# Sends of routed rows in the experts' first blocks: two behind step seven, none at step six and behind step two

## The chip, the cores and the metric

The kernel runs on one core of a Trainium2 chip. The metric is the time of one launch on the device in microseconds (us), lower is better. A core has five engines that run side by side, each through its own instructions in order: TensorE (PE, with its weight loads shown apart as PEld), VectorE (DVE), ScalarE (ACT), GpSimd (POOL) and SyncE (SP). They wait for each other by semaphores. DMA transfers are issued here by SP, POOL and ACT.

## The reference

```python
def reference(**kwargs):
    # x: (8, 5056, 128), h: (5056, 128)
    Yf = rfft(x, n=2 * S, axis=1) * rfft(h, n=2 * S, axis=0)   # a long causal convolution
    x = irfft(Yf, n=2 * S, axis=1)[:, :S].reshape(40448, 128)
    g = argmax(x @ w_group)             # one of 4 groups, softmax weight g_w
    e = argmax(x @ w_expert[g])         # one of 4 experts in it, softmax weight e_w
    out[token] = g_w * e_w * (relu(x[token] @ w1[g, e]) @ w2[g, e])
```

Each of the 40448 rows of the convolution's result thus goes through one of 16 experts (128 to 1024 to 128), all in float32.

## The kernel before

**Two halves that overlap.** The convolution is done in three rounds of three sequences (`ROUNDS`; one of the nine is `h`). The end of a round, its last transform and the routing of its rows, is `side(r)`: eight parts, of which each has two *lumps* on PE, further pieces of PE work (logits, transposes: `lm`, `lt`, `rows`), some 40 small DVE steps (`gate_math`) and at its end 15 *sends* (10 in the first round). A lump (`lump`, L721 and L735) is 48 and 24 matmuls of small size into the banks `py0` and `py1`, which ACT then copies to `yT` (L742). The experts are worked off in blocks of 512 rows, gathered by expert in the DRAM tensor `srt`.

**A send.** `scatter` (from L849 on) makes a function for each column of 128 rows; `send` (L869) takes the oldest from the list `self.sends` and calls it, or does nothing if the list is empty. It casts one column of positions to integers (L853: on DVE, or on ACT if asked by `send("s")`) and then has POOL issue an indirect DMA that writes these rows to `srt` (L854). `drain` sends all that is left, with casts on DVE. `rows(0)` of a part first sends what is left of the parts before the last one.

**The order is written by hand.** `run` fills the list `main` with functions; their order is the order of emission, and so the order on each engine. The blocks of the experts come in eight steps each: `step(i)` of `ffn_steps` does three matmuls of the first layer for each 128 of the inner 1024 (L1350 to L1352), three of the second for an earlier step (L1368 to L1370), ACT and DVE take the result out of PSUM as `h` (L1355, L1356), and what `PLAN` lists for the place (`act`): splits of weights and rows, and under the letter "o" the store of results: at steps 4 and 6 of the first blocks a `put` and a `send("s")`, at 3 and 5 a `scatter_out` (POOL again, L1421).

**The weave.** `weave` walks through `main`. Only steps 2 and 6 of a block have a weight (`FW`), and the large pieces of `side(2)` are emitted by weight: right behind step 2 or step 6, ahead of the next entry of `main`. So a send that is an entry of its own behind step 2 (`k % 8 == 2`) is emitted behind the large piece that follows that step, while a send within step 6 is emitted ahead of the piece that follows it. In blocks 0 to 23 sixteen lumps are emitted in this way, the first behind step 6 of block 1, the other fifteen behind steps 2; behind the steps 6 of later blocks come the other large pieces. In numbers of steps, counted from step 0 of block 0, the lumps stand behind 14, 18, 34, 42, 58, 66, 82, 90 and so on by turns of 8 and 16 to 186.

**When the list fills.** At step 0 of block 0 the list holds 14 sends of the second round. The eight parts of the third round add 15 each behind steps 42, 66, 90, 111, 135, 158, 182 and 206. `drain` stands behind steps 15 and 255; the loads of rows behind it (`ffn_x`, L1253, by SP) wait for the scatters to have landed.

Of the kernel before, what the change touches and what calls it, by code (L numbers as in the profile page):

```python
# [81 lines left out]
NA = (NTOK_A - NE * (BLK - 1) + BLK - 1) // BLK  # L82
# [139 lines left out]
def width(j):  # L222

    return BLK if j < T0 else TB if j < H0 else HB


def steps_of(n):
    return 8 // (512 // n)


class Kernel:
# [1245 lines left out]
    def ffn_steps(self, j, prev, end):  # L1477

        n = width(j)
        ns = steps_of(n)  # L1480
        plan = PLAN[n]

        def bank(j):
            return (NW_MIN - 1 - j) % 2 if j < NW_MIN else 0

        def behind(i):

            if j < NW_MIN:
                return [i - 2]
            return [] if i < 3 else [ns - 4, ns - 3] if i == ns - 1 else [i - 3]  # L1490

        def loads_a():
            if j + 2 < end:
                self.ffn_x(j + 2)

        def loads_w():
            if j + 2 < end:
                self.ffn_w(j + 2)

        def act(at):  # L1500
            for w, k, q in plan:
                if w != at:
                    continue
                if q == "w":
                    loads_w()
                elif q == "s":
                    if prev:
                        self.out_store(
                            prev[0], self.blk[j - 1]["ids"] if prev[1] is None else prev[1], j - 1 if j < NW_MIN else None
                        )  # L1510
                elif q == "o":
                    if prev and j < NA - 2 and at in (4, 6):
                        self.put()
                        self.send("s")
                    elif prev:
                        self.scatter_out(1 if ns == 8 else 4, j < NW_MIN)
                elif j + k < end and (j + k, q) not in self.kept:
                    if q == "x":
                        self.ffn_prep_x(j + k)
                    else:  # L1520
                        self.ffn_prep_w(j + k, q)

        def step(i):
            def f():
                if i == 0:
                    loads_a()
                act(i - 0.5)
                if i >= 2 or j not in (T0, H0):
                    self.mm1(j, i)
                if i >= 2:  # L1530
                    for q in behind(i):
                        self.mm2(n, q, bank(j), j)
                elif prev:
                    self.mm2(prev[0], steps_of(prev[0]) - 2 + i, bank(j - 1))
                    if i == 1:
                        self.out_evac(prev[0], bank(j - 1))
                act(i)

            return f

        return [step(i) for i in range(ns)]
# [81 lines left out]
    def run(self):  # L1623
        tc = self.tc
        with ExitStack() as ctx:
            self.pools(ctx)
            with ExitStack() as c2:
# [10 lines left out]
                def add(f, w=0.0):  # L1638
                    main.append((w, f))
# [4 lines left out]
                def advance(g):  # L1644
                    return lambda: next(g, None)
# [50 lines left out]
                for k, f in enumerate(steps):  # L1696
                    for g in rest[LATE * k:LATE * k + LATE]:
                        add(g)
                    if k == 8 * (N0 - 2) - SIDE1:
                        mark["end", 1] = len(main)  # L1700
                    if k == START2 - 7:
                        add(side[2][0])
                    if k == START2:
                        mark["start", 2] = len(main)
                    if 8 * (N0 - 2) - SIDE1 < k:
                        for _ in range(NTA):
                            add(advance(ta))
                    if k == 8 * (NA - 2) - SIDE2:
                        mark["end", 2] = len(main)
                    if 8 * (NA - 2) - SIDE2 < k < 8 * NA:  # L1710
                        for _ in range(NTA):
                            add(advance(tq))
                    if 8 * NA <= k:
                        add(advance(tb))
                    if 8 * NA + FILL <= k:
                        add(advance(fill))
                    if 8 * NW_MIN - AHEAD <= k:
                        add(advance(ahead))
                    if k < 4:
                        add(lambda q=(0, 2, 1, 3)[k]: self.ffn_w(1, (q,)))  # L1720
                    add(f, FW[k % 8])
                    if k in (8 * (N0 - 2) - 1, 8 * (NA - 2) - 1):
                        add(self.drain)
                    elif k < 8 * (NA - 2) and k % 8 not in (3, 4, 5, 6):
                        add(lambda: self.send("s"))
                    elif k >= 8 * (NA - 2) and k % 8 in (7, 0, 1, 2):
                        add(lambda: self.scatter_out(1, True))
                    if k % 8 == 6:
                        add(lambda: (self.due.extend(self.taken), self.taken.clear()))
                    m, n = k // 8 - NA, (PUT1 - PUT0) // 2  # L1730
                    if k % 8 == 0 and 0 <= m < TAKE and (m + 1) * n // TAKE > m * n // TAKE:
                        add(lambda i=m * n // TAKE: self.take(i))
# [31 lines left out]
```

## Time and profile before

| | us |
|---|---|
| median of 3 runs | 1758.63 |
| shortest and longest of them | 1750.66, 1761.71 |
| the profiled execution | 1759.51 |
| its span, first to last instruction | 1757.7 |

The span is what the trace covers; the profiled execution's own time is 1.8 us more. Busy times are those of instructions on an engine. Matmuls overlap, and their ends are modelled, so a short wait between two of them can hide under the shown length of the first; where that matters, the length of a whole stretch is taken. "issue" as the cause of idle time means that the engine waited for nothing that the profile shows.

### The profile page before, as it was taken

To read this page: it belongs to the slowest core of one execution; us is meant where nothing else is said; L and a number is where in the kernel's file an instruction comes from. 1 tells how busy PE (TensorE), PEld (TensorE's weight loads), DVE (VectorE), ACT (ScalarE), POOL (GpSimd) and SP (SyncE) were. 2 spreads that over 40 slices of the span, in tenths; PEclk is the share of its full clock that TensorE was granted. 3 is DMA by queue.
4 is the path that set the end of the run, shared out by engine and by line. 5 is a ranking of instruction groups with operands and counts; after the bars stand their busy time and mean duration, and the time that the engine had idled before them with its cause. 6 is when DMAs were issued, how large, how long until landed. Compare 5 with 4: busy or idle time off the path is not lost. (4 is left out here: it accounts for less than half of the span.)

```text
span 1757.7 us, 48202 instructions
## 1 busy us (share of the span) xinstructions
PE 1661.5 (95%) x16765; PEld 1299.0 (74%) x16765; DVE 1297.0 (74%) x3080; ACT 1043.0 (59%) x2461; POOL 769.0 (44%) x742
## 2 busy tenths in 40 slices
PE   8998899988898998999999999999999999999997
PEld 8677756567655556777777778787788877888987
DVE  6554598864586787777777778887787778877876
ACT  5564444443343445666666666676666666666765
POOL 1451243442454454144455545254565554334444
PEclk9999999999998999999999999999999999999999
DMA  7796677876487777555665654447545584444554
GB/s 219 229 299 204 179 249 237 275 230 182 145 247 232 244 226 212 168 165 163 171 175 167 171 152 147 133 144 227 186 148 156 166 254 136 130 129 146 156 164 152
DMA packets 281640, 330.26 MB, mean 188 GB/s; under 512 B 33335, under 2 KB 216000, under 8 KB 281368
## 3 DMA queue, kind: packets, MB, share of 16 engines
q1 hardware_dynamic: 252504, 271.00, 52.2%
q0 software_dynamic: 20608, 41.79, 6.9%
q10 hardware_dynamic: 8256, 14.10, 2.8%
q8 instruction: 140, 2.29, 0.6%
q14 instruction: 132, 1.08, 0.2%
HBM read 230.41 MB, written 96.86 MB: 186 GB/s over the span
## 5 line engine op out<-in xcount | busy, mean ns | idle before, releaser
L854 POOL DMA_INDIRECT srt<-rw,pos x320 | 344.9, 1078 | 450.0 <-DVE pos L853 173.4
L1421 POOL DMA_INDIRECT out<-orow,at x176 | 182.2, 1035 | 254.4 <-ACT at L1419 200.8
L539 DVE TENSOR_TENSOR y<-pp,hg 128x768 f32<-128x768 f32 (+1 forms) x120 | 103.8, 865 | 79.1 <-ACT hg L529 31.1
L1421 POOL DMA_INDIRECT out<-orow,sids x92 | 94.0, 1022 | 116.8 <-DVE orow L1388 83.7
L589 PE MATMUL pp<-y,cg 64*64 64x384 f32 (+1 forms) x1472 | 118.7, 444 | 14.4 <-DVE m L539 10.6
L599 ACT COPY zs<-pp 128x768 f32<-128x768 f32 (+1 forms) x118 | 85.2, 722 | 79.2 <-PE pp L589 40.2
L439 DVE TENSOR_TENSOR st<-pp,odd 128x320 f32<-128x320 f32 x90 | 44.2, 491 | 104.3 <-ACT odd L438 102.4
L521 PE MATMUL pp<-st,cg 64*64 64x192 f32 (+1 forms) x1556 | 117.8, 407 | 0.8 <-issue 0.4
L721 PE MATMUL py<-ig,zm 126*64 126x79 f32 x2048 | 95.5, 243 | 18.7 <-issue 15.1
L721 PEld LDWEIGHTS py<-ig,zm 126*64 126x64 f32 x2048 | 82.1, 142 | 39.2 <-issue 28.0
L1356 DVE SCALAR_TENSOR_TENSOR h0l<-px,h0h 128x512 fp32r<-128x512 f32 (+1 forms) x109 | 73.5, 675 | 50.1 <-ACT h0h L1355 34.9
L742 ACT COPY yT<-py 128x474 f32<-128x474 f32 (+1 forms) x96 | 44.6, 513 | 106.2 <-PE py L735 86.6
L1355 ACT ACTIVATE h0h<-px 128x512 fp32r<-128x512 f32 (+1 forms) x109 | 63.9, 586 | 73.6 <-PE px L1352 47.3
L539 DVE TENSOR_TENSOR m<-pp,hg 128x768 f32<-128x768 f32 (+1 forms) x120 | 102.9, 858 | 1.2 <-ACT hg L531 1.2
L1356 DVE SCALAR_TENSOR_TENSOR h2l<-px,h2h 128x512 fp32r<-128x512 f32 (+1 forms) x112 | 75.5, 674 | 37.8 <-ACT h2h L1355 28.9
L589 PEld LDWEIGHTS pp<-y,cg 64*64 64x64 f32 x1472 | 59.2, 133 | 53.4 <-issue 26.7
L1356 DVE SCALAR_TENSOR_TENSOR h3l<-px,h3h 128x512 fp32r<-128x512 f32 (+1 forms) x111 | 74.6, 672 | 30.2 <-ACT h3h L1355 26.8
L521 PEld LDWEIGHTS pp<-st,cg 64*64 64x64 f32 x1556 | 62.9, 134 | 40.3 <-issue 33.6
L1355 ACT ACTIVATE h3h<-px 128x512 fp32r<-128x512 f32 (+1 forms) x111 | 65.2, 587 | 37.3 <-PE px L1352 27.1
L573 POOL TENSOR_TENSOR y<-y,m 128x512 f32<-128x512 f32 x40 | 51.0, 1276 | 74.5 <-DVE m L561 42.0
L1356 DVE SCALAR_TENSOR_TENSOR h1l<-px,h1h 128x512 fp32r<-128x512 f32 (+1 forms) x111 | 74.7, 673 | 8.3 <-issue 2.9
L1355 ACT ACTIVATE h1h<-px 128x512 fp32r<-128x512 f32 (+1 forms) x111 | 65.1, 587 | 22.1 <-PE px L1352 10.0
(476 smaller groups left out, 5187.4 us busy)
## 6 DMA issues: line engine op xcount, KB each, us to landing
wr<-in_moe_w SPq DMA_DIRECT2D x373, 256.0 KB
zd<-zs SPq DMA_DIRECT2D x78, 384.0 KB
zm<-zd SPq DMA_DIRECT2D x64, 378.0 KB
cg<-in_c_g SPq DMA_DIRECT2D x102, 224.0 KB
xr<-srt SPq DMA_DIRECT2D x71, 260.0 KB
hg<-hd SPq DMA_DIRECT2D x80, 128.0 KB
zd<-zs SPq DMA_DIRECT2D x39, 256.0 KB
xt<-in_x ACTq DMA_DIRECT2D x54, 160.0 KB
```

The lines of the kernel that those rows point to most:

```text
L439: nc.vector.tensor_tensor(out=all_st[:, 0:2 * HALF, d], in0=even, in1=odd, op=ALU.add)
L521: nc.tensor.matmul(px[c * 64:c * 64 + 64, b, to], lhsT=k, rhs=data[:, of], start=begin, stop=i == len(steps) - 1 or p == 0 and i == 1, til ...
L539: nc.vector.tensor_tensor(out=t[:, :, 0:w].rearrange("p t (r u d) -> p t r u d", r=2, u=nu), in0=taken(px, part).unsqueeze(1).broadcast_to ...
L573: (nc.gpsimd if r == 0 else nc.vector).tensor_tensor(out=y[:, :, 0:w], in0=y[:, :, 0:w], in1=m[:, :, 0:w], op=ALU.add)
L589: nc.tensor.matmul(pz[c][h:h + 64, 0:w], lhsT=wt[c * 64:c * 64 + 64, k + h:k + h + 64], rhs=y[c * 64:c * 64 + 64, part, 0:w], start=part = ...
L599: nc.scalar.copy(out=z[:, 0:n, 0:w], in_=pp[:, 0:n, 0:w])
L721: nc.tensor.matmul(pys[q][c:c + 64, col(n, u)], lhsT=zms[q][:, n % QB, k:k + 64], rhs=self.ig[:, 0:NH], start=n % QB == 0 and u == 0, stop ...
L742: nc.scalar.copy(out=self.yT[:, k:k + QB * c1], in_=pys.pop(q)[:, 0:QB * c1])
L854: ins = self.nc.gpsimd.indirect_dma_start(out=self.srt, out_offset=bass.IndirectOffsetOnAxis(ap=k["pos"][0:p, j:j + 1], axis=0), in_=k["rw ...
L1355: nc.scalar.activation(out=hh, in_=p, func=AF.Relu)
L1356: nc.vector.scalar_tensor_tensor(out=hl, in0=p, scalar=0.0, in1=hh.bitcast(F32), op0=ALU.max, op1=ALU.subtract)
L1421: ins = self.nc.gpsimd.indirect_dma_start(out=self.a["out"], out_offset=bass.IndirectOffsetOnAxis(ap=ids, axis=0), in_=o, in_offset=None, ...
```

## The change

One entry of `PLAN` keeps its `put` at step 6 and loses its send; behind step 2 there is no send any more; behind step 7 there are two. Where a list of sends is empty, a call does nothing, as before. So a block that follows another has five places for a send (7, 7, 0, 1 and within 4) where it had six (7, 0, 1, 2 and within 4 and 6).

```diff
                     if prev and j < NA - 2 and at in (4, 6):
                         self.put()
-                        self.send("s")
+                        if at == 4:
+                            self.send("s")
                     elif prev:
                         self.scatter_out(1 if ns == 8 else 4, j < NW_MIN)
...
                     add(f, FW[k % 8])
                     if k in (8 * (N0 - 2) - 1, 8 * (NA - 2) - 1):
                         add(self.drain)
-                    elif k < 8 * (NA - 2) and k % 8 not in (3, 4, 5, 6):
+                    elif k < 8 * (NA - 2) and k % 8 in (7, 0, 1):
                         add(lambda: self.send("s"))
+                        if k % 8 == 7:
+                            add(lambda: self.send("s"))
```

`N0` is 4 and `NA` is 34 here.

## Rows read from the trace of the kernel before

**Rows 1.** The page's first part: the span, and of each engine the busy time in us, its share of the span and the number of its instructions.

```profile
span 1757.7 us, 48202 instructions
...
PE 1661.5 (95%) x16765; PEld 1299.0 (74%) x16765; DVE 1297.0 (74%) x3080; ACT 1043.0 (59%) x2461; POOL 769.0 (44%) x742
```

**Rows 2.** Busy time of each engine by stretch (the windows view; us from the span's start; length of the stretch, then busy us and instruction count of PE, PEld, DVE, ACT, POOL, then granted clock, DMA share, GB/s): all before the turn to the experts, the stretch in which the last 120 sends run, and the stretch behind it.

```profile
0.00:652.00 652.00, 587.20 (x10344) 417.62 (x10348) 440.34 (x1152) 298.97 (x773) 253.01 (x254) 0.97 0.74 226
...
754.00:1092.00 338.00, 335.87 (x2372) 269.18 (x2371) 259.93 (x600) 230.85 (x575) 175.98 (x166) 1.00 0.58 164
1092.00:1500.00 408.00, 400.49 (x1872) 323.99 (x1871) 323.28 (x684) 281.66 (x652) 200.93 (x192) 1.00 0.56 170
```

**Rows 3.** Who PE waited for between 720 and 1095 us (the waits view: what waited, for whom, us in total, times, the longest in us); these four lines are the whole answer.

```profile
PE py L721 <- issue: 1.1, 3, 0.4
PE py L735 <- issue: 0.4, 1, 0.4
PE ptr L1370 <- DMA wr<-in_moe_w: 0.3, 1, 0.3
PE pz L1370 <- issue: 0.3, 1, 0.3
```

**Rows 4.** The windows view again, one stretch for each of the twelve lumps that had a scatter on POOL beside them: it begins with the lump's first L721 matmul and ends where PE takes up the next step (columns as in rows 2, so the fifth pair is the busy time of POOL in the lump and the count of its instructions that fall in it). The last line sums the columns.

```profile
694.04:697.95 3.91, 3.33 (x74) 2.69 (x73) 1.31 (x3) 0.71 (x4) 1.95 (x2) 1.00 0.79 255
703.63:707.42 3.79, 3.48 (x74) 2.64 (x73) 1.29 (x2) 0.64 (x3) 1.93 (x2) 1.00 0.18 54
779.35:782.77 3.42, 3.07 (x74) 2.56 (x73) 3.35 (x11) 0.86 (x2) 1.66 (x2) 1.00 0.29 72
825.34:828.79 3.45, 3.12 (x73) 2.63 (x72) 3.23 (x12) 0.65 (x2) 1.00 (x2) 1.00 0.33 75
871.64:874.40 2.76, 2.76 (x74) 2.45 (x73) 2.64 (x11) 0.07 (x1) 0.97 (x1) 1.00 0.28 64
886.60:889.46 2.86, 2.86 (x73) 2.55 (x72) 1.74 (x3) 1.53 (x4) 0.98 (x1) 1.00 0.51 117
917.10:920.04 2.94, 2.94 (x73) 2.56 (x72) 2.58 (x10) 0.09 (x1) 0.96 (x1) 1.00 0.29 68
932.43:935.84 3.41, 3.02 (x73) 2.64 (x73) 1.47 (x3) 0.93 (x2) 1.41 (x2) 1.00 0.17 51
962.96:966.04 3.08, 3.08 (x73) 2.63 (x72) 2.52 (x9) 0.54 (x2) 1.00 (x1) 1.00 0.34 68
978.30:981.81 3.51, 3.13 (x73) 2.62 (x72) 1.37 (x3) 0.82 (x2) 1.30 (x2) 1.00 0.32 72
1008.90:1011.80 2.90, 2.90 (x73) 2.55 (x72) 1.81 (x7) 0.82 (x3) 1.46 (x2) 1.00 0.31 93
1023.98:1027.11 3.13, 3.05 (x74) 2.59 (x73) 1.29 (x2) 0.59 (x2) 0.98 (x1) 1.00 0.22 72
sum 39.16, PE 36.73 PEld 31.11 DVE 24.61 ACT 8.26 POOL 15.62; mean PE 3.06 PEld 2.59 DVE 2.05 ACT 0.69 POOL 1.30
```

**Rows 5.** The same for the four lumps without one.

```profile
734.57:737.32 2.75, 2.75 (x73) 2.44 (x72) 2.63 (x7) 1.28 (x3) 0.00 (x0) 1.00 0.22 38
749.51:752.26 2.75, 2.75 (x73) 2.44 (x72) 1.29 (x2) 0.53 (x2) 0.00 (x0) 1.00 0.24 39
794.95:797.71 2.76, 2.76 (x73) 2.45 (x73) 1.29 (x2) 0.54 (x2) 0.00 (x0) 1.00 0.41 80
841.09:843.84 2.75, 2.75 (x73) 2.44 (x72) 1.29 (x2) 0.53 (x2) 0.00 (x0) 1.00 0.50 113
```

**Rows 6.** The timeline of POOL around the lump at 825.34 us (start, us, engine, line, operation, out<-in, count, and in brackets the idle time before it and what ended that), and under it PE's rows of the lump in the same view.

```profile
823.10 0.98 POOL L854 DMA_INDIRECT srt<-rw,pos  x1 [2.32 <-ACT pos L853]
...
825.67 0.98 POOL L854 DMA_INDIRECT srt<-rw,pos  x1 [0.31 <-issue]
...
825.35 1.72 PE L721 MATMUL py<-ig,zm 126*64 126x79 f32 x42
827.39 0.44 PE L721 MATMUL py<-ig,zm 126*64 126x79 f32 x6 [0.33 <-issue]
```

**Rows 7.** ACT and POOL between 754 and 1092 us: the groups of the casts and of the scatters (the lines view: count | busy us, mean ns of one | idle us before them and what ended it), and one line of the waits of ACT.

```profile
L853 ACT CAST pos<-posf 128x1 int32<-128x1 f32 x120 | 23.3, 194 | 5.2 <-DVE posf L985 5.2
...
L854 POOL DMA_INDIRECT srt<-rw,pos x120 | 131.4, 1095 | 108.8 <-ACT pos L853 59.2 <-issue 19.3 <-DVE kept_ids L1398 9.7
...
ACT h0h L1355 <- PE px L1352: 10.8, 15, 2.2
```

**Rows 8.** The drain behind step 15: the timeline of POOL (first and last of its four scatters), of SP (the load of block 4's rows and the first load of its weights) and of ACT (the first use of those weights).

```profile
700.61 0.98 POOL L854 DMA_INDIRECT srt<-rw,pos  x1 [4.17 <-DVE pos L853]
...
704.69 1.17 POOL L854 DMA_INDIRECT srt<-rw,pos  x1 [0.31 <-issue]
...
707.39 0.37 SPq L1253 DMA_DIRECT2D xr<-srt  x1
708.60 0.37 SPq L1286 DMA_DIRECT2D wr<-in_moe_w  x1
...
725.01 0.61 ACT L1297 CAST w0h<-wr 128x512 fp32r<-128x512 f32 x1
```

**Rows 9.** DMA queues in the lump that begins at 825.34 us up to the end of its gap (its first line: the scatters' queue), then in the one that begins at 794.95 us (the instructions' queue): packets, MB, share of 16 engines.

```profile
q0 software_dynamic: 81, 0.17, 21.6%
...
q8 instruction: 1, 0.02, 2.4%
```

## The prediction

> **What bounds the kernel now.** I read the page's first part first: PE is busy for 1661.5 of 1757.7 us, 95% [rows 1]. Next the windows by stretch, to see where the other 5% lie. Before the turn to the experts PE has 652 - 587.2 = 64.8 us of idle time; in the stretch from 754 to 1092 us, in which all but a few of the sends that the change moves are run, it has 338 - 335.87 = 2.13 us, at a granted clock of 1.00, the upper level, 2.4 GHz [rows 2]. So the change works where PE is the bound and almost nothing is left to win: DVE is busy for 77% there, ACT for 68%, POOL for 52%. The third view, who PE waited for, says the same: 2.1 us between 720 and 1095 us, none of it put down to ACT or to POOL, 1.1 of it in the middle of lumps (L721) and for no cause that the profile shows [rows 3].
>
> Since matmuls overlap, I then took the length of each whole lump, from its first matmul to PE's next work. Here is the one thing that the change can touch. The four lumps with no scatter on POOL beside them took 2.75 to 2.76 us each, without spread [rows 5]. The twelve with one or two took 2.76 to 3.91 us, 39.16 together [rows 4]. Against 12 x 2.75 = 33.0 that is 6.16 us of PE time lost. The reader should see that the POOL count separates the two groups, but does not fix the size: with a scatter in it the lump at 871.64 us lost 0.01 us, the one at 978.30 lost 0.76. The two dearest, at 694.04 and 703.63, lost 1.16 and 1.04; the other ten lost 39.16 - 3.91 - 3.79 - 27.5 = 3.96, a mean of 0.40.
>
> **Part 1: how many sends, and when.** I counted through the order of emission. A part of the third round adds 15 sends every 21 to 24 steps, which is about three blocks. Three blocks had 18 places and now have 15. Before, the list ran empty some steps ahead of the next part; now it is empty for a step at most from step 42 on, and the last send goes out behind step 233 where it was 225. The drain behind 255 finds nothing either way, and `rows(0)` never has to send by force: when part 2 asks at step 70, the last send of part 0 went out behind step 65. The number of sends stays, so the work on ACT and POOL stays too: 23.3 us of casts and 131.4 us of scatters for the 120 of the third round [rows 7].
>
> **Part 2: what leaves step 6 and step 2.** A cast takes 0.194 us on ACT and a scatter 1.095 us on POOL [rows 7]. Neither is on PE's path: ACT waits for PE ahead of the `h0h` of a block, 10.8 us in 15 waits [rows 7], and PE waits for ACT nowhere in the stretch [rows 3]. With 36 of the 120 casts leaving these steps the most that could be in it is 36 x 0.194 = 7.0 us if all of it were on the path; I take 0, because PE has only 2.13 us of idle time there [rows 2]. What hides the casts is ACT's idle time behind PE. Were that cover gone, they would cost PE the same in the new place. The send at step 6 stands ahead of a lump only once, behind step 14 (the lump at 694.04); the other lumps stand behind steps 2, and there the send was already emitted behind the lump. So for fifteen lumps out of sixteen these removals take nothing from in front of the lump. For the first, one of its two scatters goes: 1.16 becomes the mean of lumps with one, 0.40, a gain of 0.76 us.
>
> **Part 3: two casts behind step 7.** ACT does a second cast of 0.194 us ahead of the next block's `h0h`. At 25 such places the loss is 25 x 0.194 = 4.9 us if nothing covers it, and 0 if ACT's wait for PE does. I take 0: of these 15 waits the mean is 10.8 / 15 = 0.7 us [rows 7], room for three casts. The four waits of a cast for positions that were not ready, 5.2 us of ACT in all [rows 7], go, since a new part's sends now queue behind the old ones. PE did not wait for them, so this gains 0.
>
> **Part 4: POOL ahead of a lump.** This decides the sign. Before, three scatters come in the steps ahead of a lump (7, 0, 1), back to back: 823.10 to 825.67 us is two of them in 2.57 us, 1.285 each, and the third begins 0.32 us into the lump; the lump's gap ends 0.74 us behind that scatter's end [rows 6]. Now there are four (7, 7, 0, 1), so the third takes the place that it had and the fourth begins at about 1.6 us in the lump and ends at 2.6. At the same distance its effect would come at 3.3 us, behind the end of an undisturbed lump (2.75); where the row begins earlier, it falls in. I price the fourth at half of 0.40 us. Further, the list hardly ever runs empty, so all twelve lumps from step 58 to 186 have sends ahead of them, where ten had:
>
> - the twelve: 12 x 0.40 = 4.8, against 3.96 before
> - the fourth scatter in them: 12 x 0.20 = 2.4
> - the lump at 694.04: 0.40, against 1.16
> - the lump at 703.63, beside the drain: 1.04, as before
>
> That is 8.6 against 6.16, a loss of 2.4 us. The bounds: if no scatter disturbs a lump any more, 6.2 us are won. If each of the twelve costs as much as the dearest on record, 12 x 1.16 + 1.16 + 1.04 = 16.1, some 10 us are lost. I take the value between, nearest to the ten lumps.
>
> **Part 5: the drain behind step 15.** Places at steps 2, 10 and 14 are lost and one at 7 is won, so six sends are drained, not four. The four begin at 700.61 and 704.69 us, 1.36 apart; two more end 2.7 us later. The load of block 4's rows then goes out at about 710.1 for 707.39, and the weight loads queued behind it on SP from about 711.3 for 708.60. Their first use is at 725.01 [rows 8], some 14 us on. Cost 0; with the cover gone it would be 2.7 us once. It ends below the bounds above and is in them.
>
> **A rule weighed against the rows.** In the lump at 825.34 us no instruction packet moved up to the end of its gap, while 81 packets of the scatters' queue did; in the lump at 794.95 an instruction packet moved and nothing was lost [rows 9, 5]. The Trainium skill's page "Runtime: NRT & Kernel Launch", section "Instruction fetch mechanics", says that an engine's instructions come in by DMA in blocks of 16 KiB and that this is mostly hidden. By that rule the gaps could be late refills, which a move of sends would leave in place, and the sum would be 0 in place of 2.4. The rows speak against it.
>
> **The rivals.**
>
> *The lumps are relieved.* If what counts is a send emitted just ahead of or behind a large piece, taking the sends from step 6 and from behind step 2 ends the losses: 1758.6 - 6.2 = 1752.4 us. For it: the first lump, with a send in step 6, is the dearest. Against: fifteen lumps have the same three neighbours ahead as before.
>
> *The lumps suffer more.* The fourth scatter falls in and each lump pays like those with two: 1758.6 + 9.9 = 1768.5. For it: the lumps at 694.04 and 703.63. Against: 1008.90, with two on record and a loss of 0.15 [rows 4].
>
> *Slower by more than 1%.* One mechanism: scatters inside lumps. It decides from 17.6 us on, that is (17.6 + 3.96) / 12 = 1.8 us in each of twelve lumps; the dearest on record is 1.16. It would give 1776 or more.
>
> *The gaps have nothing to do with sends.* Then the change does nothing, 1758.6. For it: the loss in a lump with scatters goes from 0.01 to 1.16 us without a visible rule. Against: none of the four lumps without a scatter lost anything [rows 4, 5].
>
> **How the numbers follow.** The sum stands against the profiled execution's 1759.51: 1761.9. The median of the runs lies 0.9 below that execution, so I predict 1761.0. About 1% (17.6 us) is what a measurement can tell from no change here. Chances: my forecast 0.50, relieved lumps 0.18, dearer lumps 0.18, nothing to do with sends 0.08, over 1% slower 0.04, and 0.02 left for a gain over 1%, for which no row has room. All but the last two are within 1%: 0.94. The range takes in both bounds, 1752.4 and 1768.5, widened by a half to 1.5 us because the runs before spread over 11 us: 1751 to 1769.
>
> **What would show it right or wrong.** PE's idle time in the stretch of the sends stays at some 2 to 5 us. Lumps from step 58 on take 2.9 to 3.6 us, those at steps 66 and 90 among them, which took 2.76 and 2.75; the first takes less than 3.9. POOL shows four scatters in a row from the end of step 7 on. Step 15 drains six, and the loads behind it go out 2 to 3 us later without a wait of PE. I am wrong if the lumps fall to 2.75 with sends ahead of them, if PE waits for an `h` behind step 7, or if the time moves while the lumps don't.

## The result, and the profile after

The changed kernel takes 1765.99 us, the median of 12 runs (1762.91 to 1771.36), against 1755.85 of the kernel before (12 runs, 1749.87 to 1761.71). The ratio is 1.0056, 95% interval 1.004 to 1.0073: it is slower by some 10 us, 0.56%. That lies in the predicted range and within 1%, but four times as far from before as the 2.4 us that were forecast. The profiled execution took 1764.85 us.

The page's first part (columns as in rows 1):

```profile
span 1763.2 us, 48202 instructions
...
PE 1669.1 (95%) x16765; PEld 1304.9 (74%) x16765; DVE 1297.1 (74%) x3082; ACT 1045.3 (59%) x2459; POOL 767.4 (44%) x742
```

As many instructions as before [rows 1]; two casts have gone from ACT to DVE, since the drain casts there. Now the stretches (columns as in rows 2): around the drain, and that of the third round's sends.

```profile
704.00:708.00 4.00, 2.74 (x25) 2.03 (x25) 0.00 (x0) 0.71 (x2) 0.83 (x1) 0.59 0.12 34
708.00:712.00 4.00, 4.00 (x12) 3.20 (x12) 1.38 (x2) 0.97 (x3) 1.00 (x1) 0.55 0.76 208
...
754.00:1092.00 338.00, 333.00 (x2351) 265.63 (x2344) 254.40 (x592) 227.98 (x559) 164.84 (x156) 1.00 0.55 160
```

In the sends' stretch PE has 338 - 333.00 = 5.0 us of idle time where it had 2.1 [rows 2], at the upper clock as before. Around the drain something is new: a granted clock of 0.59 and 0.55. Who PE waited for between 706 and 1110 us (the whole answer, columns as in rows 3):

```profile
PE py L735 <- issue: 2.5, 5, 1.0
PE py L721 <- issue: 2.4, 8, 0.4
PE py L1013 <- DVE cntc L1102: 0.7, 1, 0.7
PE ptr L1370 <- issue: 0.3, 1, 0.3
PE pz L1370 <- issue: 0.3, 1, 0.3
```

4.9 us, against 1.5 in rows 3, lie inside lumps, and for no cause that the profile shows. PE waits for ACT nowhere. So the lumps again, each from its first matmul to PE's next work: the first two, and of the twelve behind step 58 and later the first four with the sum over all twelve (columns as in rows 4):

```profile
691.44:694.25 2.81, 2.81 (x74) 2.50 (x73) 1.32 (x3) 0.51 (x2) 0.65 (x1) 1.00 0.79 225
700.31:707.31 7.00, 5.00 (x73) 3.42 (x73) 0.95 (x2) 0.16 (x2) 3.60 (x4) 0.82 0.16 50
...
781.18:785.62 4.44, 4.01 (x73) 2.83 (x72) 3.49 (x10) 1.08 (x3) 2.63 (x3) 1.00 0.25 61
797.78:801.09 3.31, 3.05 (x73) 2.59 (x73) 1.29 (x2) 0.54 (x2) 1.18 (x2) 1.00 0.30 70
828.46:832.95 4.49, 3.21 (x74) 2.76 (x73) 3.13 (x10) 0.74 (x2) 2.03 (x3) 1.00 0.16 47
845.23:848.41 3.18, 3.08 (x73) 2.63 (x72) 1.29 (x2) 0.53 (x2) 1.19 (x2) 1.00 0.37 83
...
sum 43.69, PE 39.30 PEld 32.25 DVE 24.33 ACT 6.76 POOL 20.35; mean PE 3.27 PEld 2.69 DVE 2.03 ACT 0.56 POOL 1.70
```

The twelve took 39.16 - 3.91 - 3.79 + 2.76 + 2.75 = 36.97 us before [rows 4, 5]; now 43.69. No lump of the twelve is free of loss, and those 16 steps behind the last one, as at 781.18 and 828.46, suffer most. The lump at 828.46 shows how: POOL's timeline around it, and under it PE's (columns as in rows 6).

```profile
826.21 0.98 POOL L854 DMA_INDIRECT srt<-rw,pos  x1 [3.13 <-ACT pos L853]
827.49 0.98 POOL L854 DMA_INDIRECT srt<-rw,pos  x1 [0.30 <-issue]
828.78 0.98 POOL L854 DMA_INDIRECT srt<-rw,pos  x1 [0.31 <-issue]
830.06 1.04 POOL L854 DMA_INDIRECT srt<-rw,pos  x1 [0.30 <-issue]
...
828.46 1.72 PE L721 MATMUL py<-ig,zm 126*64 126x79 f32 x43
830.42 0.40 PE L721 MATMUL py<-ig,zm 126*64 126x79 f32 x5 [0.24 <-issue]
831.86 1.16 PE L735 MATMUL py<-igt,zt 64*64 64x158 f32 x24 [1.04 <-issue]
```

Here the third and the fourth scatter have a gap of PE each: the third ends at 829.76 and PE goes on at 830.42, the fourth ends at 831.10 and PE goes on at 831.86, so 0.66 and 0.76 us behind the scatters' ends, as the 0.74 of before [rows 6]. The gap of the fourth is the longer one: 1.04 us are shown. Where the row comes earlier the lump loses less: in the six lumps behind steps 66, 90, 114, 138, 162 and 186 the fourth scatter ends 1.2 to 1.5 us behind the lump's begin, and they take 3.06 to 3.32 us; in the other six it ends at 1.7 to 3.2 us, and they take 3.57 to 4.49. The drain's lump, with six scatters behind step 15 where there were four [rows 8]; POOL's first and last, then PE:

```profile
697.41 0.98 POOL L854 DMA_INDIRECT srt<-rw,pos  x1 [5.32 <-DVE pos L853]
...
703.82 1.01 POOL L854 DMA_INDIRECT srt<-rw,pos  x1 [0.30 <-issue]
...
700.31 1.04 PE L721 MATMUL py<-ig,zm 126*64 126x79 f32 x24 [0.33 <-DMA zm<-zd]
701.67 1.00 PE L721 MATMUL py<-ig,zm 126*64 126x79 f32 x23 [0.32 <-issue]
703.06 0.27 PE L721 MATMUL py<-ig,zm 126*64 126x79 f32 x1 [0.38 <-issue]
...
704.48 0.58 PE L735 MATMUL py<-igt,zt 64*64 64x158 f32 x4 [0.42 <-issue]
705.90 1.47 PE L735 MATMUL py<-igt,zt 64*64 64x158 f32 x17 [0.84 <-issue]
...
708.65 0.63 PE L1351 MATMUL aux<-x0h,w0l 128*128 128x512 f32 x1
709.07 0.63 PE L1352 MATMUL aux<-x0l,w0h 128*128 128x512 f32 x1
...
711.85 0.40 PE L1368 MATMUL pz<-h2h,w2h 128*128 128x512 f32 x1
```

The last of these matmuls in the kernel before:

```profile
709.99 0.39 PE L1368 MATMUL pz<-h2h,w2h 128*128 128x512 f32 x1
```

PE goes on at 701.67, 703.06, 704.48 and 705.90: steps of 1.39 to 1.42 us, about one for each scatter, and only a handful of matmuls run between the last of them. The clock falls in the lump already, to 0.82 over the whole of it, and stays down behind it: the 512-column matmuls at 708.65 and 709.07 begin 0.42 us apart, at the lower level, where they begin 0.23 us apart in the kernel before. That one shows a clock of 1.00 through its drain's lump [rows 4].

The account, after against before: the twelve lumps +6.7; the drain's lump 7.00 - 3.79 = +3.2, a part of it by the clock; the first lump 2.81 - 3.91 = -1.1; the work behind the drain's lump at the lower level +2.0, since it takes 711.85 - 707.31 = 4.54 us up to the last matmul shown, where it took 709.99 - 707.42 = 2.57. Sum 10.8 us. From the begin of the first lump to the end of the last the two traces differ by as much, 1035.34 - 691.44 = 343.90 us against 1027.11 - 694.04 = 333.07, so the account leaves little out; the medians differ by 10.1. The two spans differ by only 5.5, because in this execution the stretches ahead of the first lump and behind the last were 2.6 and 2.7 us shorter than in that of the kernel before.

### The profile page after: what moved, and what is told of

Read it like the earlier page. It is cut to its first block, busy times and chain, and to the rows that moved or that the text cites. A ratio compares the mean times of both kernels' runs of the same rounds, so it can differ in the third digit from the quotient of the medians.

```text
span 1763.2 us, 48202 instructions
## 1 busy us (share of the span) xinstructions
PE 1669.1 (95%) x16765; PEld 1304.9 (74%) x16765; DVE 1297.1 (74%) x3082; ACT 1045.3 (59%) x2459; POOL 767.4 (44%) x742
## 5 line engine op out<-in xcount | busy, mean ns | idle before, releaser
L589 PE MATMUL pp<-y,cg 64*64 64x384 f32 (+1 forms) x1472 | 122.3, 453 | 13.4 <-DVE m L539 9.5
L521 PE MATMUL pp<-st,cg 64*64 64x384 f32 (+1 forms) x1556 | 118.8, 406 | 2.3 <-PE pp L521 0.9
L721 PE MATMUL py<-ig,zm 126*64 126x79 f32 x2048 | 92.9, 238 | 17.8 <-issue 12.4
L721 PEld LDWEIGHTS py<-ig,zm 126*64 126x64 f32 x2048 | 79.5, 139 | 39.0 <-issue 28.9
```

The costliest lines, as they stand in the source:

```text
L521: nc.tensor.matmul(px[c * 64:c * 64 + 64, b, to], lhsT=k, rhs=data[:, of], start=begin, stop=i == len(steps) - 1 or p == 0 and i == 1, til ...
L589: nc.tensor.matmul(pz[c][h:h + 64, 0:w], lhsT=wt[c * 64:c * 64 + 64, k + h:k + h + 64], rhs=y[c * 64:c * 64 + 64, part, 0:w], start=part = ...
L721: nc.tensor.matmul(pys[q][c:c + 64, col(n, u)], lhsT=zms[q][:, n % QB, k:k + 64], rhs=self.ig[:, 0:NH], start=n % QB == 0 and u == 0, stop ...
```

## The experiments

The expectations name three theories. The first: scatters ahead of and in the lumps cost PE its time, the fourth of them most. The second: the two casts behind step 7 hold ACT, and ACT holds PE. The third: the drain's lump is all of it. Experiments come in three groups of kernels, each on one chip with runs of the kernel before beside them (1754.86 us in the first group, the median of 21 runs). The edits are those of the kernel before unless another is named.

**No send behind step 2** (`e2_no2`; places 7, 0, 1 and within 4 and 6).

```diff
-                    elif k < 8 * (NA - 2) and k % 8 not in (3, 4, 5, 6):
+                    elif k < 8 * (NA - 2) and k % 8 in (7, 0, 1):
```

> Only the send behind step 2 is taken out (places 7, 0, 1 and within 4 and 6); step 6 keeps its send and step 7 has one. Six sends are left for the drain behind step 15, as in the changed kernel. Theory A (PE loses time in a lump by each scatter that POOL runs just ahead of it or in it): three sends ahead of each of twelve lumps, so some 0.4 us each as before, 4.8 in all against 4.0; the drain's lump near 7 us as in the changed kernel; together 4 to 6 us over the kernel before, ratio 1.002 to 1.004. Theory B (the second cast behind step 7 makes ACT late for the next block and PE waits): no second cast, ratio 1.000. Theory C (all of the loss is the longer drain behind step 15): ratio as the changed kernel's, 1.005.

Measured: 1756.06 us (12 runs), ratio 1.0003 (0.9987 to 1.0018). Two things cancel in it. The twelve lumps fall to 35.0 us, 2.0 less than before. In every second one of them POOL's row now ends 0.3 to 0.9 us ahead of the lump, and the one scatter in the lump comes after a pause: the lump at 933.19 takes 2.76 us, where its counterpart at 932.43 took 3.41 with part of a second scatter in it [rows 4]. The drain has six scatters here too, and its lump takes 6.74 us. So the drain's loss comes with the removal of the sends behind step 2. The first theory's ratio, 1.002 to 1.004, was missed, because it had the twelve lumps at 4.8 us of loss and they lost 2.0. The ratio alone is the second theory's; what speaks against that theory is the changed kernel, in which PE waits for ACT nowhere.

**A second send behind step 7, nothing else** (`e3_two7`; places 7, 7, 0, 1, 2 and within 4 and 6).

```diff
                         add(lambda: self.send("s"))
+                        if k % 8 == 7:
+                            add(lambda: self.send("s"))
```

> Only the second send behind step 7 is added (7, 7, 0, 1, 2 and within 4 and 6). The drain behind step 15 has three sends where the kernel before has four; the list runs empty sooner, so that six lumps have four sends ahead, three have two or three and the others none. Theory A: the six lose 0.9 to 1.3 us each, all twelve some 7 to 8 us against 4.0, the drain's lump 1 us or less: 2 to 4 us over the kernel before, ratio 1.001 to 1.002. Theory B: 17 second casts, most of the changed kernel's loss, ratio 1.003 to 1.005 and waits of PE for ACT behind steps 7. Theory C: a shorter drain, ratio 0.999.

Measured: 1769.48 us (6 runs), 1.0079 (1.0063 to 1.0095), worse than the whole change and a miss for all three theories. Six lumps with four scatters ahead of them take 3.91 to 4.62 us; between them the list runs empty, and the other six take 2.75 to 2.81. The twelve sum up to 42.95, 6.0 more than before; the drain's lump, with three scatters, falls to 2.76. The six took 2.76 to 3.51 us before, with three; each grew by 1.0 to 1.2 us, which is the price of the fourth scatter where it falls in whole. The rest of the 14.6 us is not all placed: at 1095 us ACT sat for 3.61 us ahead of an `h0h`, in a row of scatters without a pause on POOL, and with the lower clock behind it (0.62 between 1102 and 1106 us) PE lost some 4 us there against the trace of before. That is a hold-up that no theory foresaw.

**The changed kernel with the old places in blocks 0 and 1** (`e4_first`; four scatters drained).

```diff
-                        self.send("s")
+                        if at == 4 or j < 2:
+                            self.send("s")
...
-                    elif k < 8 * (NA - 2) and k % 8 not in (3, 4, 5, 6):
+                    elif k < 8 * (NA - 2) and k % 8 in ((7, 0, 1, 2) if k < 16 else (7, 0, 1)):
                         add(lambda: self.send("s"))
+                        if k % 8 == 7 and k >= 16:
+                            add(lambda: self.send("s"))
```

> The changed kernel, but blocks 0 and 1 keep the old places, so that the drain behind step 15 has four sends as in the kernel before and the first lump its send in step 6. Theory A: the twelve later lumps as in the changed kernel (43.7 us, 10.7 lost against 4.0), the drain's lump back at 3.8 us and no drop of the granted clock there: 6 to 7 us over the kernel before, ratio 1.003 to 1.004. Theory B: as the changed kernel, 1.005. Theory C: 1.000.

Measured: 1762.87 us (10 runs), 1.0043 (1.0027 to 1.0058). The drain's lump takes 3.70 us, 0.72 of them a wait for a load (`zm`), and the clock does not fall; the twelve lumps take 44.0, as in the changed kernel. 44.0 - 37.0 = 7.0 of its 8.0 us are lumps. So the drain is not all of it: the third theory falls, and the drain is the smaller part.

**From block 2 on sends only behind steps 3 to 7** (`e5_quiet`; none just ahead of or behind a lump).

```diff
-                        self.send("s")
+                        if j < 2:
+                            self.send("s")
...
+                    elif k < 8 * (NA - 2) and k % 8 in ((7, 0, 1, 2) if k < 16 else (3, 4, 5, 6, 7)):
```

> Five sends in a block as in the changed kernel, but behind steps 3, 4, 5, 6 and 7, none behind 0, 1 and 2; blocks 0 and 1 keep the old places. POOL has then worked off the last scatter before the next lump begins. Theory A: the twelve later lumps take 2.75 to 2.8 us each, 4 us under the kernel before, ratio 0.997 to 0.998. Theory B: one cast behind step 7, ratio 1.000. Theory C: 1.000. If the gaps in lumps have nothing to do with sends: lumps stay at 2.76 to 3.5 us and the ratio at 1.000.

Measured: 1773.6 us (5 runs), 1.0105 (1.0089 to 1.0121), a miss. The lumps do what was expected, all twelve take 2.75 to 2.76 us, and yet it is the slowest of all. PE now waits for ACT, and ACT for nothing that is late. ACT's timeline and POOL's at one such place:

```profile
1080.31 0.18 ACT L853 CAST pos<-posf 128x1 int32<-128x1 f32 x1
1084.81 0.60 ACT L1355 ACTIVATE h0h<-px 128x512 fp32r<-128x512 f32 x1 [4.32 <-PE px L1352]
...
1079.99 1.21 POOL L854 DMA_INDIRECT srt<-rw,pos  x1 [0.30 <-issue]
1081.51 0.97 POOL L854 DMA_INDIRECT srt<-rw,pos  x1 [0.30 <-issue]
1082.79 0.98 POOL L854 DMA_INDIRECT srt<-rw,pos  x1 [0.30 <-issue]
```

The matmul that `h0h` needs is followed by others of PE until 1083.86; it ended at about 1081.1, and ACT began 3.7 us later, 1.0 us behind the end of the last scatter of a row of seven without a pause. Set against the trace of before, matmul by matmul, PE loses some 21 us outside the lumps between blocks 2 and 28, in steps of 0.4 to 2.9 us, and wins 3.5 in them. So scatters packed between lumps move the loss from PE to ACT. What holds ACT was not found.

**Which part of a send does it: four kinds of extra work.** Four kernels are the kernel before with extra work that the result doesn't need: ahead of the lumps behind steps 34, 42, 66 and 90, four extra pieces each, of one kind per kernel. Before each, ACT copies a 128 x 128 tile.

```diff
+        if kind == "scatter":    # d_scatter: POOL, a DMA by index
+            nc.gpsimd.indirect_dma_start(out=to, out_offset=..., in_=dm, ...)
+        elif kind == "plain":    # d_plain: POOL, a plain DMA
+            nc.gpsimd.dma_start(out=to, in_=dm)
+        elif kind == "sp":       # d_sp: SP, the same DMA
+            nc.sync.dma_start(out=to, in_=dm)
+        else:                    # d_pool: three adds on POOL, no DMA
+            for _ in range(3):
+                nc.gpsimd.tensor_tensor(out=dm, in0=dm, in1=self.ident, op=ALU.add)
...
+                    if k in (31, 32, 33, 39, 40, 41, 63, 64, 65, 87, 88, 89):
+                        for _ in range(2 if k % 8 == 7 else 1):
+                            add(lambda: self.dummy(kind))
```

> The kernel before, with extra work that the result doesn't need: ahead of the lumps behind steps 34, 42, 66 and 90, which have no send ahead of them and take 2.75 us, four scatters of 128 rows of 512 bytes to a scratch tensor, two behind step 7 and one each behind steps 0 and 1, each released by a copy on ACT. If it is the scatter on POOL that costs PE (theory A), the four lumps take 3.1 to 4.6 us as lumps with four sends ahead do. If it is the state of the list or the casts of positions, they stay at 2.75.

> The same places and bytes, but the copy to the scratch tensor is a plain DMA issued by POOL in place of a scatter by index. If what costs is POOL making and posting a software DMA, the four lumps take 3.1 us or more here too; if it takes the indices, they stay at 2.75.

> The same places, but in place of each scatter three adds of 128x128 on POOL and no DMA. If a busy POOL, its reads of SBUF or the extra copy on ACT are what costs, the four lumps grow; theory A expects 2.75 to 2.8, since no DMA is made.

> The same places and bytes, the copy to the scratch tensor issued by SP. If the bytes that are in flight beside the lump cost PE its time, whoever issues them, the four lumps grow as with the scatters; theory A expects 2.75 to 2.8.

Measured, one run each: 1685.19, 1689.89, 1682.52 and 1683.33 us, on a chip on which the kernel before took 1687.96, some 68 us less than on the others. There the question could not be put. Of `d_scatter`, the lump of the drain and two of the four lumps with extra scatters (columns as in rows 4), and under them PE's row at the gap in the drain's lump:

```profile
647.79:651.14 3.35, 2.97 (x73) 2.54 (x72) 1.29 (x2) 0.53 (x2) 1.93 (x2) 1.00 0.22 67
678.48:681.24 2.76, 2.76 (x73) 2.44 (x72) 2.28 (x6) 1.68 (x5) 1.95 (x2) 1.00 0.34 78
...
738.17:740.93 2.76, 2.76 (x74) 2.45 (x73) 1.29 (x2) 0.54 (x2) 2.15 (x3) 1.00 0.50 93
...
649.21 1.04 PE L721 MATMUL py<-ig,zm 126*64 126x79 f32 x24 [0.38 <-DMA zm<-zd]
```

With two and three scatters in it a lump takes 2.76 us. The drain's lump takes longer, but by the profile its gap ends with the landing of a load. No loss beside scatters is seen on this chip, and the four kernels tell nothing apart. So two of them were run again elsewhere.

**The same on a third chip, and the change beside it.** The changed kernel as it is (`after2`), to see that the loss is there:

> The changed kernel again, unaltered. The four runs with extra work ran on another chip than the runs before them; there the kernel before took 1687.96 us and no lump after the drain's lost anything beside its scatters. Theory A with this condition (a chip on which the kernel before takes some 1755 us loses PE time to scatters in lumps, one on which it takes some 1688 us doesn't): if the kernel before takes 1750 to 1762 here, the ratio is 1.004 to 1.007 and the twelve lumps take 43 to 44 us; if it takes some 1688, the ratio is 0.999 to 1.002 and they take 33.1. If the loss is the same on every chip: 1.004 to 1.007 either way.

1763.68 us (7 runs) against 1753.58 of before (16 runs): 1.0063 (1.0031 to 1.0095). Its twelve lumps take 44.1 us, the drain's 7.13 (0.63 of them a wait for a load). The loss is there.

> The kernel with four extra scatters ahead of the lumps behind steps 34, 42, 66 and 90, unaltered, to read it on the chip on which the changed kernel is read in the same call. Where the changed kernel's twelve lumps take 43 us, the four take 3.1 to 4.6 us if scatters are the cause, and 2.76 if the list of sends or the casts of positions are. Where the changed kernel's take 33.1, the four take 2.76 again.

> The kernel with adds on POOL in place of the extra scatters, unaltered, for the same reason. Theory A: 2.76 on every chip. If a busy POOL or the extra copies on ACT cost PE: over 3 us where the changed kernel's lumps grow.

One run each: 1766.36 and 1757.57 us. Of `d_scatter2`, the first and the last of the four lumps and the sum over them:

```profile
733.71:737.57 3.86, 3.52 (x73) 2.89 (x73) 3.34 (x9) 1.68 (x4) 1.94 (x2) 1.00 0.18 56
...
844.54:851.24 6.70, 4.16 (x73) 3.42 (x72) 1.29 (x2) 1.10 (x2) 2.54 (x3) 0.89 0.26 70
sum 19.72, PE 14.21 PEld 11.79 DVE 7.90 ACT 5.49 POOL 8.13; mean PE 3.55 PEld 2.95 DVE 1.98 ACT 1.37 POOL 2.03
```

And of `d_pool2`, the first of the four and the sum over them; POOL is as busy in them, but issues at most one scatter in each:

```profile
735.85:738.60 2.75, 2.75 (x73) 2.44 (x72) 2.27 (x6) 1.67 (x4) 2.59 (x5) 1.00 0.23 30
...
sum 11.03, PE 11.03 PEld 9.79 DVE 6.70 ACT 3.24 POOL 9.97; mean PE 2.76 PEld 2.45 DVE 1.67 ACT 0.81 POOL 2.49
```

19.7 us against 11.0, same chip, same copies on ACT, POOL busy for 8.1 us in the one and 10.0 in the other. So it is the scatters, not a busy POOL, nor the extra copies ahead of them. Whether a plain DMA issued by POOL or by SP would do the same on a chip that shows the loss was not tried. Bytes in flight alone are not enough: in the kernel before the lump at 841.09 us took 2.75 with 113 GB/s moving and no scatter in it [rows 5], and the one at 828.46 in the changed kernel took 4.49 with 47.

**From block 2 on no send behind step 1** (`e9_relief`; places 7, 0, 2 and within 4 and 6: two scatters ahead of a lump instead of three).

```diff
-                    elif k < 8 * (NA - 2) and k % 8 not in (3, 4, 5, 6):
+                    elif k < 8 * (NA - 2) and k % 8 in ((7, 0, 1, 2) if k < 16 else (7, 0, 2)):
```

> From block 2 on the send behind step 1 is taken out of the kernel before, so that two scatters (behind 7 and 0) run ahead of a lump and are over when it begins; places 7, 0, 2 and within 4 and 6, five in a block. Blocks 0 and 1 as before. Theory A: the twelve lumps take 2.76 to 2.9 us, 33.1 to 34.8 in all, 3 to 4 us less than the kernel before where it loses 4.0 (ratio 0.998), the same where it loses nothing (1.000). A rival: as with the sends behind 3 to 7, POOL's row of scatters reaches into other places and ACT is held up at a block's start, ratio over 1.003.

Measured: 1750.92 us (10 runs), 0.9983 (0.9962 to 1.0005). One of its lumps and the sum over the twelve:

```profile
927.09:929.85 2.76, 2.76 (x73) 2.45 (x73) 1.29 (x2) 0.58 (x2) 0.00 (x0) 1.00 0.56 149
...
sum 33.10, PE 33.10 PEld 29.36 DVE 23.65 ACT 8.82 POOL 1.15; mean PE 2.76 PEld 2.45 DVE 1.97 ACT 0.74 POOL 0.10
```

All loss is gone from the twelve: 37.0 - 33.1 = 3.9 us, where the 37.0 is from the trace of the first group's kernel before. The median falls by 2.7, and the interval just takes in no change, so a gain is not shown. It is the lowest median of the chips with a loss, and its distance from before is of the size that these lumps had to give: 3.96 by the prediction's list.

## Why the prediction was right in its range and short in its size

**What bounds the kernel** held: PE is the bound, and the change acts only through lumps. With `e9_relief` on one side and the changed kernel on the other, the same sends cost these twelve lumps nothing or 10.7 us (43.69 - 33.0) by their place alone.

**The range was wide, and luck helped the number.** 1751 to 1769 takes in a gain of 6 us and a loss of 10, so the result could lie in it without the sum being right. The forecast of 1761.0 also stood on a median of three runs, 1758.63, where twelve give 1755.85: the time is missed by 5.0 us, the change by 10.1 - 2.4 = 7.7.

**Part 1** held. The list hardly runs empty, and the lumps behind steps 66 and 90, without scatters before, take 3.31 and 3.18 us (797.78 and 845.23).

**Parts 2 and 3**, the casts at 0, held: PE waits for ACT nowhere in the changed kernel, so two casts behind step 7 cost nothing there, and the second theory falls. The first lump gained 1.1 us for a forecast of 0.76.

**Part 4 failed in size.** The twelve lumps were forecast at 4.8 + 2.4 - 3.96 = 3.2 us more and cost 6.7. The step that failed is "At the same distance its effect would come at 3.3 us, behind the end of an undisturbed lump (2.75)", and with it the price of half of 0.40 us for the fourth scatter. The distance was right: in the lump at 828.46 PE goes on 831.86 - 828.46 = 3.40 us behind its begin. But this is where a gap ends, and I took it for where it acts. The gap itself is long, begins inside the lump, and the third scatter's gap had by then pushed the lump's work back. `e3_two7` has the price alone: a fourth scatter makes lumps of 3.91 to 4.62 us, 1.0 to 1.2 us each more than the same lumps before, for a forecast of 0.20. Ten lumps with one or two scatters beside them were no measure for a row of four, since their mean of 0.40 mixed two kinds. In five (779.35, 825.34, 932.43, 978.30 and 1023.98) the third scatter of a row begins 0.2 to 1.0 us behind the lump's begin, and they lost 0.38 to 0.76; in the other five it begins ahead of the lump, or the row is shorter, and they lost 0.01 to 0.33 [rows 4]. That is also the rule that the prediction missed in the losses from 0.01 to 1.16.

**Part 5 failed in one line.** The loads behind the drain went as told: counted from the lump's begin, the load of block 4's rows goes out at 707.52 - 700.31 = 7.2 us where it went out at 3.8 [rows 4, 8], and nobody waits for it.

```profile
707.52 0.37 SPq L1253 DMA_DIRECT2D xr<-srt  x1
```

What failed is "the lump at 703.63, beside the drain: 1.04, as before" of Part 4's list, and "Cost 0" with it. I followed the two added scatters to SP's queue and not to the lump, in which both lie. They cost 3.2 us there and 2.0 behind it, by the clock.

**The rule weighed** was rightly set aside. DMA queues of the changed kernel between 829 and 832 us, over the longest gap of the lump shown:

```profile
q0 software_dynamic: 95, 0.20, 20.1%
```

It is the only queue that moved packets: no instruction packet, as in rows 9. The Trainium skill's page "Runtime: NRT & Kernel Launch", section "Instruction fetch mechanics", has instructions come in by DMA in blocks of 16 KiB; if the gaps were late refills, such a block would have to land in them, and the trace speaks against that a second time.

**The rivals.** *The lumps suffer more* was the case, at 1768.5 for 1765.99 measured. It had the mechanism, though it priced each lump like the two dearest of before; the twelve lost (43.69 - 33.0) / 12 = 0.89 each, and the drain's lump, which it held at 1.04, and the clock made up for that. So its number came out close in part by two errors that cancel. *The lumps are relieved* was wrong for this change, which puts four scatters where three were; `e9_relief` shows that it is the right aim. *Nothing to do with sends* falls with `d_scatter2` against `d_pool2`. *Over 1%* would have needed 1.8 us in each lump.

**Open.** Why a scatter stops PE between small matmuls was not found; that it is the scatter is shown, by what path is not, nor what of it does it (the issue on POOL, or the packets that follow). Nor is it known what holds ACT in `e5_quiet` and `e3_two7`, nor whether it is the same thing.

## What to carry to other kernels

Where one engine issues DMAs by index back to back, look at what the busiest engine does up to 1.2 us behind the end of each: a stall there has no releaser in the profile, and only the length of a whole stretch, sorted by how many such issues lie in it, shows it. When work is taken from one place, follow it to where it piles up (here a drain right ahead of a lump), on every engine and not on its own queue alone. Price a longer row of a disturbing operation from rows of that length, or give it the dearest case: the mean over short rows is no estimate of it.

## What the runs showed of the hardware that was not expected

**Gaps behind the scatters, and growing.** In the last lump of `d_scatter2` shown above, five scatters end at 842.51, 843.79, 845.10, 846.41 and 847.69 us, and two more came ahead of these. PE:

```profile
844.54 1.17 PE L721 MATMUL py<-ig,zm 126*64 126x79 f32 x27
846.08 0.36 PE L721 MATMUL py<-ig,zm 126*64 126x79 f32 x4 [0.37 <-issue]
847.50 0.30 PE L721 MATMUL py<-ig,zm 126*64 126x79 f32 x2 [1.06 <-issue]
848.91 0.77 PE L721 MATMUL py<-ig,zm 126*64 126x79 f32 x15 [1.11 <-issue]
```

PE goes on 0.98, 1.09 and 1.22 us behind the last three ends, where it was 0.66 and 0.76 for a row of four, and runs four and two matmuls in between. Gaps and scatters do not always pair off: in the lump at 826.71 us of `e3_two7` scatters end at 828.01 and 829.36, and PE stands still three times and goes on at 828.70, 829.44 and 830.17.

**It depends on the chip.** On the chips of the first and the last group of kernels it is seen. On that of the four kinds the same lumps with as many scatters took 2.75 us, and the kernel before 1687.96 us instead of 1754.86 and 1753.58. What differs there is unknown. Most of the 68 us lie elsewhere: the drain's lump begins at 647.79 us in `d_scatter` and at 703.63 in the kernel before [rows 4].

**SP is held up too, on the same chips.** At the line of a weight load SP runs a MOVE of 29 ns. In the changed kernel some take 0.7 us, in `d_scatter`, on the chip without losses, none does (count: shortest/median/longest in ns, first and last start; the changed kernel first):

```profile
L1288 SPq MOVE wr<-in_moe_w x187: 2/29/717, 658.0 to 1750.5; - x187
...
L1288 SPq MOVE wr<-in_moe_w x187: 29/29/29, 605.7 to 1671.1; - x187
```

Of SP's 490 MOVEs in the changed kernel 24 took over 0.4 us, and each of them ended less than 1.5 us behind the end of a scatter on POOL. In the four kernels on the chip without losses none did. So PE is not the only engine that is held up beside scatters; whether the cause is the same is not shown.

**The clock fell in lumps with many gaps.** In the drain's lump, in which PE stood still again and again, the granted clock came down to the lower level (0.82 over the lump), and behind it matmuls of 512 columns began 0.42 us apart instead of 0.23. `e2_no2`, with a lump of 6.74 us in the same place, shows it as well (0.71 between 708 and 712 us), and so does the last lump of `d_scatter2` shown above (0.89). `e4_first`, with a lump of 3.70 us in the drain's place, shows no fall.
